# Attention decode on one Trainium2 core: a unit's scores summed in the bank they are made in

## The chip, the core and the metric

The kernel runs on one core of one Trainium2 chip. Its engines are PE (matrix products), DVE (vector), ACT (scalar), POOL (gpsimd) and SP, whose queue issues nearly all transfers; 16 DMA engines move the data from HBM. PE writes to PSUM, which has banks of 128 rows by 512 fp32 values; everything else lies in SBUF, also with 128 rows (partitions). The metric is the device time of one execution in microseconds. Three runs of the kernel before took 217.59 us in the median (217.28 to 218.31).

## The reference

All values are fp32. Two tokens (batch B = 2, one position each, D = 512) attend with 32 query heads of 128 channels over 8 key/value heads, four query heads to each, over the last 4096 positions of the cache. A gated MLP on the same input makes the gate.

```python
def reference(x, k_cache, v_cache, wq, wo, w_in, w_sp, b_sp, w_out):
    xn = layernorm(x)                                  # 2 x 1 x 512
    q = (xn @ wq) as 2 x 32 x 1 x 128
    k, v = the last 4096 positions of the caches, each head repeated 4 times
    p = softmax(q . k * 128 ** -0.5)
    s = (p . v) as 2 x 1 x 4096 @ wo
    z = gelu(xn @ w_in); z1, z2 = halves of z; z2 = layernorm(z2)
    g = silu((z1 * (w_sp * z2 + b_sp)) @ w_out)
    return x + s * g
```

K and V together are 2 x 8 x 4096 x 128 values each, 33.6 MB apiece. With the weights the kernel reads 89.40 MB.

## The kernel before

The work of attention is cut into eight **units**, one for each pair of key/value heads of a token. A unit's K is 128 partitions by 64 positions by 128 channels (one load of 4096 KB), and its V the same; a partition holds 64 neighbouring positions of one of the two heads.

**Transfers.** `ring` has four slots of 4 MB. `enqueue` (L85) and `advance` (L92) hand the slots out in a fixed order: Wq (two slots), w_in, w_out, K0, K1, V0, K2, V1, K3, and so on to K7, V6, V7, and then the output weights wo in pieces of 16, 8, 4, 1, 1, 1 and 1 blocks. A load is issued on SP's queue as soon as the work that read the slot before it is done: from K3 and V2 on, K of unit n+2 after the four transposes of unit n, and V of unit n+2 after the values product of unit n. The queue takes its loads one after the other.

**A unit's scores.** `turn(u, m)` (L371), for m = 0 to 3, is one DVE transpose of 32x32 blocks over 16 of the 64 positions; it makes `kt`, with three buffers. After it, channels lie within blocks of 32, and a product has to be taken for each quarter of 32 channels (`dq`), with its own stationary operand `q_of(u, dq)`, 32 columns wide. `shares` (L378) takes the four products of one key quarter m, one for each `dq`, each into its own group of 32 rows of one PSUM bank `sh`, with nothing summed; ACT copies the bank to SBUF as `shs`. `add_shares` (L389) then sums the four row groups and puts them in their place with a full-width product by the 0/1 matrix `add_dq`: with `add_dq` shifted by m columns, query column 16a + 4g + h of quarter m lands in row 32g + 16a + 4h + m. Four such products, summed in a bank `s`, make a unit's scores. An fp32 product is two passes on PE, and the profile has a record for each.

**The rest of a unit** is done one unit later. `share_max` (L395) finds the maxima (`m2`, `mg`, `mo`, `mx`, `nb`), `probs` (L410) takes the exponentials on ACT with their sums, `probs_t` transposes them, `values` (L436) makes 16 products with V into four row groups of `acc`, `scale_out` and `collect` gather the result.

**The order** is the program's: the engines' calls go through `InOrder` (L27), and the loop at L493 writes each engine's order out by hand. In a turn of the loop with unit u and the unit before it, prev: transpose 0 and its scores; maximum and exponentials of prev; transpose 1, its scores and the sum of quarter 0; values of prev; transposes, scores and sums of the others; the last sum; gathering of prev. After the loop come the last unit's maximum, exponentials and values (L521 to L536), and then the product with wo (L540 to L556): 28 blocks into `part`, which is copied and spread into `so`, and the last four blocks straight into `so`. Two vector operations and the store end the kernel.

Of the kernel before, what the change touches and what calls it, by code (L numbers as in the profile page):

```python
# [9 lines left out]
F32 = mybir.dt.float32  # L10
AF = mybir.ActivationFunctionType
# [3 lines left out]
P = 128  # L15
HQ, DH = 32, 128
G = 4
# [4 lines left out]
def ap(t, offset, dims):  # L22

    return bass.AP(tensor=t.tensor, offset=t.offset + offset, ap=[list(t.ap[0])] + [list(d) for d in dims])
# [18 lines left out]
def kernel(  # L43
# [13 lines left out]
    nc = tc.nc  # L57
    pe, dve, act, sp = (InOrder(tc, e) for e in (nc.tensor, nc.vector, nc.scalar, nc.sync))
    B, _, D = x.shape
    _, HKV, SK, _ = k_cache.shape  # L60
    W = min(4096, max(256, SK // 4))
    REP = HQ // HKV
# [8 lines left out]
    JC = 512 // 32  # L71
    NCH = J // JC
# [4 lines left out]
    sb = ctx.enter_context(tc.tile_pool(name="sb", bufs=2))  # L77
# [23 lines left out]
    def const(name, *shape):  # L101
        return cst.tile([P, *shape], F32, tag=name, name=name)

    def bank(name, tag):
        return ps.tile([P, 512], F32, tag=tag, name=name, bufs=BANKS[tag])
# [75 lines left out]
    nc.gpsimd.memset(hT, 0.0)  # L181
    x4 = const("x4", DC)
    nc.gpsimd.memset(x4, 0.0)
    add_dq = const("add_dq", NCH - 1 + P)
    nc.gpsimd.memset(add_dq, 0.0)
    sel = const("sel", 56)
    nc.gpsimd.memset(sel, 0.0)
    sel4 = const("sel4", 3 + 32)
# [62 lines left out]
    nc.gpsimd.tensor_mul(perm, ap(rowm, 0, [[1, 32], [0, G]]), ap(grpm, 0, [[0, 32], [1, G]]))  # L251
    perm = perm.rearrange("p h e -> p (h e)")
    for a in range(2):
        nc.gpsimd.tensor_copy(
            ap(add_dq, NCH - 1 + 16 * a, [[32, G], [4, REP]]),
            rowm[:, 16 * a : 16 * a + 16].rearrange("p (g h) -> p g h", g=G),
        )
    am = const("am", 2)
    dve.tensor_reduce(am, rowm.rearrange("p (a x) -> p a x", a=2), axis=AX.X, op=ALU.add)
    negm = const("negm", 2)  # L260
# [33 lines left out]
    def q_of(u, dq):  # L294
        return ap(qbd, (u.n * 4 + dq) * 32, [[1, 32]])
# [74 lines left out]

    def turn(u, m):  # L371

        u.kt[m] = sb.tile([P, JC, DH], F32, tag="kt", name=f"kt{u.n}_{m}", bufs=3)
        dve.transpose(
            u.kt[m].rearrange("p j d -> p (j d)"), u.k[:, JC * m : JC * m + JC, :].rearrange("p j d -> p (j d)")
        )

    def shares(u, m):  # L378

        u.sh = bank(f"sh{u.n}_{m}", "sh")  # L380
        for dq in range(4):
            pe.matmul(
                u.sh[32 * dq : 32 * dq + 32, :], q_of(u, dq), u.kt[m][:, :, 32 * dq : 32 * dq + 32],
                start=True, stop=True,
            )
        u.shs[m] = sb.tile([P, 512], F32, tag="shs", name=f"shs{u.n}_{m}")
        act.activation(u.shs[m], u.sh, AF.Copy)

    def add_shares(u, m):  # L389

        if m == 0:
            u.s = bank(f"s{u.n}", "s")
        pe.matmul(u.s, add_dq[:, NCH - 1 - m : NCH - 1 - m + P], u.shs[m], start=(m == 0), stop=(m == NCH - 1))

    def share_max(u):  # L395
        m2 = sb.tile([P, 2], F32, tag="m2", name=f"m2_{u.n}")
# [95 lines left out]
    last = units[-1]  # L492
    for u in units:  # L493
        turn(u, 0)
        shares(u, 0)
        if old is not None and old.n == NU // B - 1:
            divide(0, gather(0))
        if prev is not None:
            share_max(prev)
            probs(prev)  # L500
        turn(u, 1)
        shares(u, 1)
        add_shares(u, 0)
        if prev is not None:
            probs_t(prev)
            weigh(prev)
            if u is not last:
                values(prev)
        for m in range(2, NCH):
            turn(u, m)  # L510
            shares(u, m)
            add_shares(u, m - 1)
        if u is not last and prev is not None:
            scale_out(prev)
        advance(u.slot["k"])
        add_shares(u, NCH - 1)
        if u is not last and prev is not None:
            advance(prev.slot["v"])
            collect(prev)
        old, prev = prev, u  # L520
# [68 lines left out]
```

## Time and profile before

| What | Before |
|---|---|
| Three runs, median (lowest to highest) | 217.59 us (217.28 to 218.31) |
| Profiled execution, first to last instruction (span) | 215.6 us |
| Runs' median less the span | 2.0 us |
| Busy: PE, DVE, ACT, POOL | 144.9, 107.1, 43.7, 4.2 us |
| Read from HBM | 89.40 MB, 415 GB/s over the span |
| Mean granted clock of PE | 0.885 |

The profiled execution has no time of its own on the page beside its span, so the span is set against the runs' median: 2.0 us lie outside it. The DMA row of the page counts how busy the 16 DMA engines are in 40 equal slices of the span, in tenths. A row of a group of instructions gives line, engine, operation, the tile written and those read, shapes and count, then busy time and the mean of one in ns, and the idle time of the engine just before them with what ended it. In a timeline a row begins with its start and its length in us. A row of a window gives the stretch, busy times of PE, PE's weight loads, DVE, ACT and POOL with counts, PE's granted clock, the DMA engines' share and GB/s. All operations stand under line 37, the helper that issues them, so they are told apart by their tiles.

### The profile page before, as it was taken

Reading aid. Unit: us, or ns where it says so; the run is one execution under the profiler, and the core shown is the slowest. Engines: PE = TensorE matmul, PEld = TensorE weight load, DVE = VectorE, ACT = ScalarE, POOL = GpSimd, SP = SyncE. Lnnn points to the kernel's source line nnn. Section 1 sums busy time; section 2 is a strip of 40 time slices with the busy share of each in tenths; the row PEclk is TensorE's granted clock in tenths of the full one; section 3 lists DMA queues with packets and bytes.
Section 4 is the critical chain, followed back from the end, with each engine's and each line's share of the span. In section 5 each row is a group of like instructions: output and inputs, shape, how many; then the busy total and the mean of one; then the engine's idle time right before and its main releaser. Section 6 shows DMA issues by size and latency. Waiting matters only on the chain.

```text
span 215.6 us, 2181 instructions
## 1 busy us (share of the span) xinstructions
PE 144.9 (67%) x848; PEld 40.3 (19%) x848; DVE 107.1 (50%) x161; ACT 43.7 (20%) x108; POOL 4.2 (2%) x22
## 2 busy tenths in 40 slices
PE   0010787224595897699599499459949967987663
PEld 0010222100021222122122132112202211222311
DVE  1140025633995943953936663793585089233101
ACT  2030000331124115114303304130331231241001
POOL 6010000000000000000000000000000000000000
PEclk9999999658599699699799789859975996999998
DMA  9898999999999999999999999999999999999990
GB/s 389 390 389 389 431 423 459 435 438 421 450 395 474 395 453 419 444 432 425 439 404 450 419 444 429 432 432 419 444 413 447 425 432 444 425 435 404 410 376 33
DMA packets 3788, 89.52 MB, mean 415 GB/s; under 512 B 434, under 2 KB 450, under 8 KB 964
## 3 DMA queue, kind: packets, MB, share of 16 engines
q1 hardware_dynamic: 3772, 89.40, 96.9%
q8 instruction: 6, 0.10, 0.2%
q14 instruction: 2, 0.02, 0.0%
q10 hardware_dynamic: 8, 0.00, 0.0%
HBM read 89.40 MB, written 0.00 MB: 415 GB/s over the span
## 4 chain that ended last, share of the span: by engine, by line
DMA 41%; PE 39%; DVE 16%; ACT 2%; issue 2%; DVEq 0%
DMA ring<-in_A_wo_dram 20%; PE sh L37 11%; DMA ring<-in_A_k_cache_dram 11%; DVE kt L37 10%; DMA ring<-in_A_wq_dram 10%; PE s L37 10%; PE acc L37 7%; PE q_ps L37 4%; PE y L37 2%; PE z L37 1%; PE col L37 1%; PE mo L37 1%; DVE gate L37 1%; DVE u L37 1%; DVE qm L37 1%
## 5 line engine op out<-in xcount | busy, mean ns | idle before, releaser
L37 DVE STREAM_TRANSPOSE kt<-ring 128x2048 f32<-128x2048 f32 x32 | 72.2, 2286 | 24.9 <-DMA ring<-in_A_k_cache_dram 24.9
L37 PE MATMUL sh<-kt,qbd 128*32 128x512 f32 x256 | 43.6, 725 | 27.0 <-DVE kt L37 27.0
L37 ACT ACTIVATE shs<-sh 128x512 f32<-128x512 f32 x32 | 19.1, 597 | 99.4 <-PE sh L37 99.4
L37 PE MATMUL s<-shs,add_dq 128*128 128x512 f32 x64 | 39.0, 716 | 0.0
L37 PE MATMUL acc<-ring,pT 128*32 128x512 f32 x256 | 31.3, 614 | 0.0
L37 PEld LDWEIGHTS s<-shs,add_dq 128*128 128x128 f32 x64 | 11.0, 215 | 30.9 <-issue 26.5
L37 PEld LDWEIGHTS sh<-kt,qbd 128*32 128x32 f32 x256 | 7.0, 117 | 46.3 <-issue 38.3
L37 PE MATMUL q_ps<-ring,xnT 128*32 128x512 f32 x64 | 8.8, 713 | 7.6 <-DMA ring<-in_A_wq_dram 7.6
L37 PEld LDWEIGHTS acc<-ring,pT 128*32 128x32 f32 x256 | 7.8, 112 | 22.3 <-issue 17.6
L37 DVE TENSOR_REDUCE m<-s 128x2 f32<-128x512 f32 x8 | 5.4, 680 | 13.0 <-PE s L37 12.9
L37 PE MATMUL xnT_ps<-ident,xn 2*128 2x2 f32 x4 | 0.6, 252 | 14.5 <-DVE xn L37 14.5
L37 ACT ACTIVATE o<-acc,diag 128x128 f32<-128x128 f32 x30 | 8.6, 374 | 4.9 <-PE acc L37 4.9
L37 PE MATMUL part<-ring,oT 128*32 128x512 f32 x56 | 6.6, 597 | 3.5 <-DMA ring<-in_A_wo_dram 3.5
L37 ACT ACTIVATE p<-s,nb 128x256 f32<-128x256 f32 x16 | 7.6, 488 | 6.6 <-DVE nb L37 6.4
L37 DVE STREAM_TRANSPOSE qT<-q_ps 128x512 f32<-128x512 f32 x2 | 1.4, 717 | 14.4 <-PE q_ps L37 14.3
L37 PE MATMUL col<-o,sel 128*32 128x512 f32 x14 | 7.3, 601 | 0.0
L37 DVE TENSOR_TENSOR res<-so,gate 128x128 f32<-128x128 f32 x1 | 0.3, 292 | 11.5 <-PE so L37 11.5
L37 DVE STREAM_TRANSPOSE pT<-p 128x512 f32<-128x512 f32 x8 | 5.4, 674 | 1.2 <-ACT p L37 1.2
L37 PE MATMUL y<-ring,hT 128*32 128x512 f32 x14 | 3.3, 996 | 3.8 <-DVE hT L37 3.8
L37 ACT ACTIVATE zs<-z 128x448 f32<-128x448 f32 x1 | 0.5, 544 | 24.7 <-PE z L37 24.7
L37 ACT ACT_TABLE_LOAD x4 | 5.1, 1283 | 0.8 <-PEq L575 0.7
L37 PEld LDWEIGHTS q_ps<-ring,xnT 128*32 128x32 f32 x64 | 2.5, 130 | 13.1 <-issue 13.1
(114 smaller groups left out, 62.2 us busy)
## 6 DMA issues: line engine op xcount, KB each, us to landing
ring<-in_A_k_cache_dram SPq DMA_DIRECT2D x8, 4096.0 KB, 20.0
ring<-in_A_v_cache_dram SPq DMA_DIRECT2D x8, 4096.0 KB, 28.1
ring<-in_A_wo_dram SPq DMA_DIRECT2D x1, 4096.0 KB, 33.2
ring<-in_B_w_in_dram SPq DMA_DIRECT2D x1, 3584.0 KB, 17.1
ring<-in_A_wo_dram SPq DMA_DIRECT2D x1, 2048.0 KB
ring<-in_B_w_out_dram SPq DMA_DIRECT2D x1, 1792.0 KB, 21.0
ring<-in_A_wo_dram SPq DMA_DIRECT2D x1, 1024.0 KB
ring<-in_A_wo_dram SPq DMA_DIRECT2D x4, 256.0 KB, 17.6
```

What stands on the lines that cost most here:

```text
L37: return self.tc.keep_in_program_order(call(*args, **kwargs))
```

## The change

A unit's score products now all go into one bank. `scores(u, ms)` takes the place of `shares`: for each channel quarter `dq` and each key quarter m of `ms` a product goes into row group m of the unit's `sh`, and the four `dq` are summed there by the accumulation of PSUM. It is called twice a unit, with m = 0, 1 after transpose 1 and with m = 2, 3 after transpose 3. `by_key_group(u)` takes the place of the four `add_shares`: one ACT copy of the full bank and one product by the 0/1 matrix `regroup`, which moves row 32m + 16a + 4g + h to row 32g + 16a + 4h + m of `s`, the place that it had before. `regroup` is copied from columns of the identity on gpsimd, where `add_dq` was cleared and filled. `kt` has four buffers instead of three. Nothing else is changed; the transfers on SP's queue stand in the same order with the same waits.

```diff
-    add_dq = const("add_dq", NCH - 1 + P)
-    nc.gpsimd.memset(add_dq, 0.0)
+    regroup = const("regroup", G, 2, REP, NCH)
...
     for a in range(2):
-        nc.gpsimd.tensor_copy(
-            ap(add_dq, NCH - 1 + 16 * a, [[32, G], [4, REP]]),
-            rowm[:, 16 * a : 16 * a + 16].rearrange("p (g h) -> p g h", g=G),
-        )
+        nc.gpsimd.tensor_copy(regroup[:, :, a], ap(ident, 16 * a, [[4, G], [1, REP], [32, NCH]]))
+    regroup = regroup.rearrange("p g a h m -> p (g a h m)")
...
-        u.kt[m] = sb.tile([P, JC, DH], F32, tag="kt", name=f"kt{u.n}_{m}", bufs=3)
+        u.kt[m] = sb.tile([P, JC, DH], F32, tag="kt", name=f"kt{u.n}_{m}", bufs=4)
...
-    def shares(u, m):
-
-        u.sh = bank(f"sh{u.n}_{m}", "sh")
+    def scores(u, ms):
+
+        if ms[0] == 0:
+            u.sh = bank(f"sh{u.n}", "sh")
         for dq in range(4):
-            pe.matmul(
-                u.sh[32 * dq : 32 * dq + 32, :], q_of(u, dq), u.kt[m][:, :, 32 * dq : 32 * dq + 32],
-                start=True, stop=True,
-            )
-        u.shs[m] = sb.tile([P, 512], F32, tag="shs", name=f"shs{u.n}_{m}")
-        act.activation(u.shs[m], u.sh, AF.Copy)
-
-    def add_shares(u, m):
-
-        if m == 0:
-            u.s = bank(f"s{u.n}", "s")
-        pe.matmul(u.s, add_dq[:, NCH - 1 - m : NCH - 1 - m + P], u.shs[m], start=(m == 0), stop=(m == NCH - 1))
+            for m in ms:
+                pe.matmul(
+                    u.sh[32 * m : 32 * m + 32, :], q_of(u, dq), u.kt[m][:, :, 32 * dq : 32 * dq + 32],
+                    start=(dq == 0), stop=(dq == 3),
+                )
+
+    def by_key_group(u):
+
+        sh = sb.tile([P, 512], F32, tag="shs", name=f"shs{u.n}")
+        act.activation(sh, u.sh, AF.Copy)
+        u.s = bank(f"s{u.n}", "s")
+        pe.matmul(u.s, regroup, sh, start=True, stop=True)
...
         turn(u, 0)
-        shares(u, 0)
...
         turn(u, 1)
-        shares(u, 1)
-        add_shares(u, 0)
+        scores(u, (0, 1))
...
         for m in range(2, NCH):
             turn(u, m)
-            shares(u, m)
-            add_shares(u, m - 1)
+        scores(u, (2, 3))
...
-        add_shares(u, NCH - 1)
+        by_key_group(u)
```

How the order moves, at three places. The digits behind a tile's name are the unit and the key quarter, and then a running number of the buffer. First PE's order in unit 1, before; `x4` is four products in a row:

```order
L37 MATMUL s0_299<-shs0_3_318,add_dq_85 128x512
L37 MATMUL sh1_0_325<-kt1_0_323,qbd_196 32x512 x4
L37 MATMUL mo0_336<-mg0_334,same_r_128 128x16
L37 MATMUL sh1_1_349<-kt1_1_347,qbd_196 32x512 x4
L37 MATMUL s1_356<-shs1_0_330,add_dq_85 128x512
L37 MATMUL acc0_360<-ring_64,pT0_358 32x512 x16
```

And in the changed kernel, from the same place:

```order
L37 MATMUL s0_308<-shs0_306,regroup_85 128x512
L37 MATMUL mo0_316<-mg0_314,same_r_127 128x16
L37 MATMUL sh1_329<-kt1_0_310,qbd_195 32x512
L37 MATMUL sh1_329<-kt1_1_327,qbd_195 32x512
L37 MATMUL sh1_329<-kt1_0_310,qbd_195 32x512
```

The scores of key quarter 0 have moved behind the maximum's product `mo` of the unit before, to those of quarter 1, and the two alternate, eight products in all ahead of `acc`. Second, PE's order in unit 7 from the scores of its third quarter on, before:

```order
L37 MATMUL sh7_2_872<-kt7_2_870,qbd_196 32x512 x4
L37 MATMUL s7_866<-shs7_1_864,add_dq_85 128x512
L37 MATMUL sh7_3_882<-kt7_3_880,qbd_196 32x512 x4
L37 MATMUL s7_866<-shs7_2_877,add_dq_85 128x512
L37 MATMUL s7_866<-shs7_3_887,add_dq_85 128x512
L37 MATMUL acc6_892<-ring_64,pT6_868 32x512 x8
```

And changed, from the last two of its eight products:

```order
L37 MATMUL sh7_767<-kt7_2_778,qbd_195 32x512
L37 MATMUL sh7_767<-kt7_3_780,qbd_195 32x512
L37 MATMUL s7_793<-shs7_791,regroup_85 128x512
L37 MATMUL acc6_795<-ring_64,pT6_776 32x512 x8
L37 MATMUL mo7_808<-mg7_806,same_r_127 128x16
```

One product by `regroup` stands where four by `add_dq` stood between the scores. Third, DVE's order at the start of the units, with what its instructions wait for, before:

```order
L37 STREAM_TRANSPOSE kt0_0_281<-ring_64 128x2048 [waits DMAHW6_49,DMAHW0_49]
L37 STREAM_TRANSPOSE kt0_1_290<-ring_64 128x2048
L37 STREAM_TRANSPOSE kt0_2_301<-ring_64 128x2048
L37 STREAM_TRANSPOSE kt0_3_311<-ring_64 128x2048 [waits DVE_49,PE_49]
L37 STREAM_TRANSPOSE kt1_0_323<-ring_64 128x2048 [waits DMAHW7_49,DVE_49,PE_49]
L37 TENSOR_REDUCE m2_0_332<-s0_299 128x2 [waits PE_49]
```

And changed:

```order
L37 STREAM_TRANSPOSE kt0_0_280<-ring_64 128x2048 [waits DMAHW6_49,DMAHW0_49]
L37 STREAM_TRANSPOSE kt0_1_282<-ring_64 128x2048
L37 STREAM_TRANSPOSE kt0_2_293<-ring_64 128x2048
L37 STREAM_TRANSPOSE kt0_3_295<-ring_64 128x2048
L37 STREAM_TRANSPOSE kt1_0_310<-ring_64 128x2048 [waits DMAHW7_49,DVE_49,PE_49]
L37 TENSOR_REDUCE m2_0_312<-s0_308 128x2 [waits PE_49]
```

The fourth transpose has lost its wait for PE; the fifth waits for PE as before, now for the product that frees the buffer of quarter 0.

## The prediction

> **What bounds the kernel now.** I read the page first: the span, the row of DMA slices and the queue table.
>
> ```profile
> span 215.6 us, 2181 instructions
> DMA  9898999999999999999999999999999999999990
> q1 hardware_dynamic: 3772, 89.40, 96.9%
> ```
>
> The 16 DMA engines are busy in every slice but the last: 89.40 MB pass through one queue, and its packets fill 96.9% of the engines' span. PE stands at 67% and DVE at 50%. Next the chain of waits, at its end:
>
> ```profile
> 168.72 33.24 DMA ring<-in_A_wo_dram
> 201.98 9.97 DMA ring<-in_A_wo_dram
> 211.99 0.47 PE so L37 x8
> ...
> 212.81 0.29 DVE res L37
> ```
>
> From 168.72 to 211.95 the chain is transfer alone; then come one product, two vector operations and the store, 3.7 us to the end of the span. So the last byte sets the end, and a change on PE or ACT moves it in two ways only: it lets the queue run empty, or it makes the work behind the last byte late. The waits say who is ahead in the steady state:
>
> ```profile
> DVE kt L37 <- DMA ring<-in_A_k_cache_dram: 24.9, 5, 8.0
> PE part L37 <- DMA ring<-in_A_wo_dram: 3.5, 3, 1.7
> ```
>
> In the later units the transposes of K wait for K to land, up to 8.0 us; compute is ahead of the transfers there. I looked for the moment of least cover in the windows from the start to each issue of a K load:
>
> ```profile
> 0.00:75.84 75.84, 34.58 (x206) 9.92 (x210) 34.65 (x74) 12.43 (x23) 4.19 (x22) 0.86 0.99 422
> 0.00:92.76 92.76, 48.72 (x278) 13.65 (x282) 45.45 (x83) 16.89 (x35) 4.19 (x22) 0.87 0.99 423
> 0.00:109.70 109.70, 62.89 (x354) 17.39 (x358) 56.35 (x93) 21.34 (x47) 4.19 (x22) 0.88 0.99 424
> 25.00:210.00 185.00, 139.73 (x796) 38.15 (x788) 102.58 (x140) 39.97 (x102) 0.00 (x0) 0.87 1.00 429
> ```
>
> The last number is GB/s. K of unit 3 goes out at 75.84, when the fourth transpose of unit 1 has freed its slot. Issued before it: Wq 8.39 MB, w_in 3.67, w_out 1.84 and five loads of 4.19, together 34.87 MB. Delivered: 422 GB/s by 75.84 us, 32.0 MB. So 2.9 MB are still queued, 6.7 us at 429 GB/s. The same sum gives 4.0 MB or 9.4 us at K of unit 4 (92.76) and 5.1 MB or 12.0 us at K of unit 5 (109.70). A unit needs 8.39 MB, 19.6 us of transfer.
>
> **The change, part by part.** Removed per unit: three of four ACT copies and three of four full-width products. The groups they come from, and the others I use:
>
> ```profile
> L37 PE MATMUL s<-shs,add_dq 128*128 128x512 f32 x64 | 39.0, 716 | 0.0
> L37 ACT ACTIVATE shs<-sh 128x512 f32<-128x512 f32 x32 | 19.1, 597 | 99.4 <-PE sh L37 99.4
> ```
>
> 24 copies of 0.597 us, 14.3 us of ACT, and 24 products of two passes each; in a row one product takes about 1.06 us, so some 25 us of PE. Neither lies on the DMA chain, so neither is a gain by itself. The gpsimd work at the start loses a memset and keeps two copies of other shape, long before their first reader at 68 us: nothing.
>
> Moved: the 16 score products of a unit. Before, four in a row went to four row groups of a bank. Now eight in a row alternate between two groups, and each group sums four products of two passes. How fast such a half is, the trace shows in another product:
>
> ```profile
> 74.46 3.64 PE L37 MATMUL acc<-ring,pT 128*32 128x512 f32 x32
> 77.92 1.04 PE L37 MATMUL sh<-kt,qbd 128*32 128x512 f32 x8
> 82.92 0.59 PE L37 MATMUL col<-o,sel 128*32 128x512 f32 x1
> 83.05 0.63 PE L37 MATMUL sh<-kt,qbd 128*32 128x512 f32 x3
> 83.35 0.59 PE L37 MATMUL col<-o,sel 128*32 128x512 f32 x1
> ```
>
> The values product puts eight passes of 512 columns on each of four groups in 3.64 us; a half puts eight on each of two. The score products now take 1.04 us for two passes on each of four. At 83.05 three passes of the next unit's scores start beside the first pass of `col`, before its second at 83.35: a group has its own line of work, and groups run beside each other. So a half should take 3.6 us at full clock, two halves 7.2 a unit, where four quarters took 4 x 1.0 and four sums 4 x 1.06. The bounds: no shorter, since a group holds eight passes; 7.2 if the two groups ran one after the other. I take 3.6, the nearest row being of the same passes and widths.
>
> [...]
>
> Where this lies on a path: **first unit**.
>
> ```profile
> 53.87 11.07 DVE L37 STREAM_TRANSPOSE kt<-ring 128x2048 f32<-128x2048 f32 x5
> 58.51 1.93 PE L37 MATMUL sh<-kt,qbd 128*32 128x512 f32 x8 [0.35 <-DVE kt L37]
> 66.50 0.69 DVE L37 TENSOR_REDUCE m<-s 128x2 f32<-128x512 f32 x1 [1.56 <-PE s L37]
> 68.53 2.31 DVE L37 STREAM_TRANSPOSE kt<-ring 128x2048 f32<-128x2048 f32 x1
> 82.96 0.69 DVE L37 TENSOR_REDUCE m<-s 128x2 f32<-128x512 f32 x1 [4.92 <-PE s L37]
> 85.44 2.31 DVE L37 STREAM_TRANSPOSE kt<-ring 128x2048 f32<-128x2048 f32 x1
> ```
>
> The first half can start where the second quarter does, 58.51. PE comes out of idling there; with 4 us at half clock it does 2.0 of its 3.6 by 62.5 and ends at 64.1. The second half ends 3.6 later, 67.7; copy 0.65 with its hand-over, regrouping 1.1: scores ready at 69.4 instead of 66.5. Queued on DVE behind that wait are the maximum, then the second transpose of unit 1 (68.53 before) and all that follows, K of unit 3 among it: 2.9 us late of 6.7 us of cover. The fourth kt buffer lets the fourth transpose go without waiting, but the fifth now waits for the whole first half; that is inside this sum.
>
> **The loop.** From 68.53 to 85.44 a unit takes 16.9 us. After the change: transpose 2.3 + 0.1, first half 5.4 (3.6 us of it at half clock), values 3.6, second half 3.6, copy and regrouping 1.75, and 2.5 from 82.96 to 85.44: 19.3 us, less where values use the idle groups. It is under the 19.6 of the transfers; each unit loses 2.4 until K is late enough to wait for: 5.3 of 9.4 us of cover at unit 4, 7.7 of 12.0 at unit 5. About 4 us of queue are left each time. No gap in the DMA, cost nothing; without that cover each late microsecond would be one of the kernel's.
>
> **The end.** After unit 7's K no load depends on its scores, but the output does.
>
> ```profile
> 172.86 2.31 DVE L37 STREAM_TRANSPOSE kt<-ring 128x2048 f32<-128x2048 f32 x1 [7.98 <-DMA ring<-in_A_k_cache_dram]
> 179.49 1.67 PE L37 MATMUL sh<-kt,qbd 128*32 128x512 f32 x8 [2.78 <-DVE kt L37]
> 179.86 4.46 DVE L37 STREAM_TRANSPOSE kt<-ring 128x2048 f32<-128x2048 f32 x2
> 188.09 1.92 PE L37 MATMUL acc<-ring,pT 128*32 128x512 f32 x16
> 200.73 0.25 DVE L37 TENSOR_SCALAR oT<-ol,wd 32x32 f32<-32x32 f32 x1
> 202.09 3.64 PE L37 MATMUL part<-ring,oT 128*32 128x512 f32 x32 [1.74 <-DMA ring<-in_A_wo_dram]
> 206.91 1.92 PE L37 MATMUL part<-ring,oT 128*32 128x512 f32 x16 [1.17 <-DMA ring<-in_A_wo_dram]
> 209.41 1.07 PE L37 MATMUL part<-ring,oT 128*32 128x512 f32 x8 [0.58 <-DMA ring<-in_A_wo_dram]
> 211.25 0.42 PE L37 MATMUL so<-parts,rowm 128*32 128x128 f32 x8
> ```
>
> Before, the scores are ready when `acc` starts, 188.09. How long PE is at half clock, the windows give:
>
> ```profile
> 160.00:166.00 6.00, 5.95 (x22) 1.33 (x26) 4.88 (x3) 0.60 (x1) 0.00 (x0) 0.50 1.02 437
> 179.40:183.10 3.70, 3.61 (x12) 0.70 (x12) 3.70 (x3) 0.60 (x1) 0.00 (x0) 0.56 1.03 443
> ```
>
> PEclk stands ahead of the DMA share: 0.56 until 183.1, once 0.50 for six busy microseconds. After the change the first half starts at 179.49, has done 1.8 of 3.6 by 183.1 and ends at 184.9; the second (transposes done at 184.3) ends by 188.5; copy and regrouping 1.75: 190.25, **2.2 us late**. Low bound 1.75, if the second half runs beside the rest of the first; high 3.4, with six microseconds at half clock. [...] What swallows it: attention is ready for the output weights at 200.98 and PE starts on them at 202.09, when they land (1.1 us); then PE waits 1.17 and 0.58 for the next pieces, and at the end 0.3 lie between the spread at 211.25 and the product on the last piece at 211.99. Together 3.15 us. So 2.2 cost nothing, 3.4 cost 0.2. V of unit 6 is weighed 2.2 later, and so the output weights' third load is issued at 194.5 instead of 192.25; it queues behind the first of them, which lands at 201.98 by the chain.
>
> The sum: nothing on the DMA chain, 0 us at the end: a span of 215.6 again, and with the 2.0 us that lie between it and the runs' median, 217.6. PE's and ACT's busy time fall without use.
>
> **The rivals.** *The two groups don't run side by side*: a half is 7.2 at full clock, the loop 2.4 + 9.0 + 3.6 + 7.2 + 1.75 + 2.5 = 26.5 us, over the transfers' 19.6; unit 1's second transpose comes at 78.7, unit 7's six loops later at 237.7 instead of 177.0, and the kernel takes about 275. For it: no row shows two groups alternating. Against: four groups do, and `col` beside three. *The clock stays at half for the whole of unit 7's scores*, since PE idles longer ahead of them: the first half ends at 186.7, the second between 191.7 and 193.9, copy and regrouping at half clock 2.75: 6.4 to 8.6 us late, over the 3.15 from which it decides; 221 to 223. Against it: in no window is PE busy at half clock for over some 6 us. *Less traffic makes the transfers quicker*: over the 29 stretches of 5 us from 55 to 200 of which these are the first and the last, the mean is 431 GB/s where PE is busier than its median and 430 where it is less:
>
> ```profile
> 55.00:60.00 5.00, 3.42 (x16) 0.43 (x16) 5.00 (x3) 0.60 (x1) 0.00 (x0) 0.50 1.03 446
> 195.00:200.00 5.00, 3.85 (x31) 1.65 (x26) 1.92 (x7) 0.63 (x2) 0.00 (x0) 1.00 0.95 410
> ```
>
> So a gain of over 1.1 us (216.4 or less) has nothing behind it. *The change doesn't shorten PE's work* (halves at half clock throughout the loop but not the end) gives the forecast's time too as long as 4 us of cover stand.
>
> **How the numbers follow.** Hidden on both sides: 0.83, 217.6, by itself 217.0 to 218.6 with the end's 0.2 and the runs' spread (217.28 to 218.31). Clock rival 0.06, serial groups 0.03, some other lateness 0.02; quicker transfers 0.06. About 0.5%, 1.1 us, is what a measurement here tells from no change. The range reaches a little to both sides, 216.6 to 219.2. Faster 0.06, same 0.83, slower 0.11.
>
> **What would show it.** In the changed profile: DMA slices full as now; the last transfer's end near 212; s with 16 passes instead of 64 and 8 copies; a half of 16 passes in 3.6 us at full clock; K of unit 3 issued near 78.7; unit 7's regrouping ended near 190; PE's waits for output weights shrunk from 3.5 us by about 2. Wrong would be a gap in the DMA row, K's wait gone in units 5 to 7, or `part` ending after 210.8.

## The result, and the profile after

The changed kernel took 219.36 us in the median of 13 runs (217.53 to 220.67), against 217.59 us for the kernel before on the same chip (217.28 to 218.31): 1.0068 times as long, with an interval from 1.0040 to 1.0096. A second series of both, on another chip, gave 218.78 us against 217.67, 1.0033 (1.0004 to 1.0061). The ratios are those of the means. So the change costs 0.3 to 0.7%, 0.7 to 1.5 us, where no change was forecast. The first median lies 0.2 us above the range that was given (216.6 to 219.2), the second inside it. That they come so near is owed to the width of the range and not to the sum, which had 0 us at the end.

The page of the changed kernel, in the rows shown of the kernel before:

```profile
span 216.1 us, 2016 instructions
DMA  9988999999999999999999999999999999999990
q1 hardware_dynamic: 3772, 89.40, 96.7%
```

The transfers look as they did: full slices, 96.7% of the engines' span against 96.9%. The chain of waits doesn't. On the page of the kernel before its shares were

```profile
DMA 41%; PE 39%; DVE 16%; ACT 2%; issue 2%; DVEq 0%
```

and on the page of the changed kernel they are, with the chain's rows at the end:

```profile
PE 54%; DVE 27%; DMA 10%; ACT 5%; issue 2%; ACTq 0%; DVEq 0%
...
204.96 6.26 PE part L37 x56
211.95 0.91 PE so L37 x24
```

Before, transfers alone made up the chain from 168.72 to 211.95. Now it runs through unit 7's scores and values into one unbroken output product of 56 passes and waits for no piece of wo. The 16 DMA engines are as busy as ever, and yet they no longer set the end. The windows around the last transfer show it, in the kernel before and then in the changed one (the last two numbers are the DMA engines' share and GB/s):

```profile
211.00:212.00 1.00, 0.79 (x26) 0.39 (x19) 0.00 (x0) 0.20 (x1) 0.00 (x0) 1.00 0.13 49
```

```profile
211.00:212.00 1.00, 0.66 (x24) 0.39 (x20) 0.00 (x0) 0.60 (x1) 0.00 (x0) 1.00 0.11 43
212.00:213.00 1.00, 0.82 (x24) 0.55 (x24) 0.12 (x1) 0.00 (x0) 0.00 (x0) 1.00 0.00 0
```

By the packets of the trace the last byte passes at 211.51 us before and at 211.39 after. Behind 212 the changed kernel has 0.82 us of PE's work left, where the chain before had one last product of 0.47 us, begun at 211.99.

What the change removed is gone as counted. The groups of the changed kernel:

```profile
L37 PE MATMUL s<-shs,regroup 128*128 128x512 f32 x16 | 9.0, 643 | 6.1 <-ACT shs L37 6.1
L37 ACT ACTIVATE shs<-sh 128x512 f32<-128x512 f32 x8 | 4.8, 597 | 34.8 <-PE sh L37 34.8
```

ACT fell from 43.7 to 30.1 us. And the vector engine's waits have changed sides:

```profile
DVE m L37 <- PE s L37: 33.8, 7, 6.3
DVE hq L37 <- PE col L37: 6.9, 2, 4.4
DVE kt L37 <- DMA ring<-in_A_k_cache_dram: 2.1, 1, 2.1
```

Before, the transposes waited 24.9 us for K: compute was ahead of the transfers. In this execution they wait 2.1 us for K and 33.8 for scores. Nothing has been lost in the transfers yet, but the lead is gone. Most of that isn't the change's doing: this execution starts its units 3.1 us later than that of the kernel before (57.0 and 53.9), for a reason that the first experiment shows, and a second profile of the same kernel, with an early start, still waits 16.3 us for K:

```profile
DVE kt L37 <- DMA ring<-in_A_k_cache_dram: 16.3, 5, 5.0
```

The first profile's timeline of unit 7 shows where the lead is missed:

```profile
172.75 2.31 DVE L37 STREAM_TRANSPOSE kt<-ring 128x2048 f32<-128x2048 f32 x1 [2.12 <-DMA ring<-in_A_k_cache_dram]
177.29 0.69 DVE L37 TENSOR_REDUCE m<-s 128x2 f32<-128x512 f32 x1 [2.23 <-PE s L37]
179.19 2.31 DVE L37 STREAM_TRANSPOSE kt<-ring 128x2048 f32<-128x2048 f32 x1
181.55 3.83 PE L37 MATMUL sh<-kt,qbd 128*32 128x512 f32 x16 [1.71 <-DVE kt L37]
186.53 3.62 PE L37 MATMUL sh<-kt,qbd 128*32 128x512 f32 x14 [1.15 <-DVE kt L37]
...
190.90 1.12 PE L37 MATMUL s<-shs,regroup 128*128 128x512 f32 x2 [0.75 <-ACT shs L37]
192.06 0.69 DVE L37 TENSOR_REDUCE m<-s 128x2 f32<-128x512 f32 x1 [5.58 <-PE s L37]
204.65 0.25 DVE L37 TENSOR_SCALAR oT<-ol,wd 32x32 f32<-32x32 f32 x1
204.96 6.22 PE L37 MATMUL part<-ring,oT 128*32 128x512 f32 x56 [0.68 <-DVE oT L37]
```

Unit 7's first transpose starts with K's landing, at 172.75, as before (172.86). The second is queued on DVE behind the maximum of unit 6, which waits 2.23 us for unit 6's scores; it starts at 179.19, and at 177.0 in the kernel before. From there to the scores' maximum it is 12.9 us, where it was 11.2 (177.0 to 188.2). 2.2 and 1.7 make attention 3.9 us late for the output weights: 204.9 instead of 200.98. In the second profile, with the early start, the second transpose comes at 178.38, and 1.34 and 1.71 make attention 3.1 us late, at 204.1. The waits of `part` for wo, 3.5 us before, are gone in both.

**The runs.** Of every run the span and PE's mean granted clock were recorded, and they say more than the medians of the times. Of the 85 runs of the kernel before that were made beside the experiments below, 83 have spans from 215.5 to 216.1 us, and two of 216.3 and 216.4. The changed kernel's 25 runs go from 215.7 to 218.9, with 217.4 in the middle, and by the clock they fall into groups: 6 runs at 0.919 to 0.921 have 215.7 to 215.9 us; 8 at 0.913 or 0.914 have 216.1 to 218.9 (seven of them 217.4 or less); 11 at 0.890 to 0.898 have 217.4 to 218.4. In the kernel before, the clock varies too (0.863 to 0.897), and the span doesn't follow it, but for the lowest clock, 0.863, where three runs have 216.1 to 216.4. So the change has laid bare PE's clock, which was hidden behind the transfers.

### The profile page after: what moved, and what is told of

Read it like the earlier page. It is cut to its first block, busy times and chain, and to the rows that moved or that the text cites. A ratio compares the mean times of both kernels' runs of the same rounds, so it can differ in the third digit from the quotient of the medians.

```text
span 216.1 us, 2016 instructions
## 1 busy us (share of the span) xinstructions
PE 148.3 (69%) x800; PEld 40.7 (19%) x800; DVE 107.1 (50%) x161; ACT 30.1 (14%) x84; POOL 4.2 (2%) x21
## 3 DMA queue, kind: packets, MB, share of 16 engines
q1 hardware_dynamic: 3772, 89.40, 96.7%
## 4 chain that ended last, share of the span: by engine, by line
PE 54%; DVE 27%; DMA 10%; ACT 5%; issue 2%; ACTq 0%; DVEq 0%
PE sh L37 23%; DVE kt L37 15%; PE acc L37 11%; DMA ring<-in_A_wq_dram 10%; PE q_ps L37 5%; PE s L37 4%; PE part L37 3%; ACT shs L37 2%; DVE m L37 2%; PE z L37 2%; PE mo L37 2%; PE y L37 2%; DVE mg L37 1%; DVE gate L37 1%; DVE u L37 1%
## 5 line engine op out<-in xcount | busy, mean ns | idle before, releaser
L37 PE MATMUL sh<-kt,qbd 128*32 128x512 f32 x256 | 75.5, 652 | 16.7 <-DVE kt L37 16.7
L37 PE MATMUL acc<-ring,pT 128*32 128x512 f32 x256 | 34.2, 595 | 0.0
L37 PEld LDWEIGHTS sh<-kt,qbd 128*32 128x32 f32 x256 | 16.3, 118 | 65.2 <-issue 35.2
L37 DVE TENSOR_REDUCE m<-s 128x2 f32<-128x512 f32 x8 | 5.5, 691 | 33.8 <-PE s L37 33.8
L37 PE MATMUL q_ps<-ring,xnT 128*32 128x512 f32 x64 | 9.9, 785 | 7.5 <-DMA ring<-in_A_wq_dram 7.5
L37 PE MATMUL s<-shs,regroup 128*128 128x512 f32 x16 | 9.0, 643 | 6.1 <-ACT shs L37 6.1
L37 PEld LDWEIGHTS acc<-ring,pT 128*32 128x32 f32 x256 | 9.2, 109 | 18.0 <-issue 17.9
L37 ACT ACTIVATE shs<-sh 128x512 f32<-128x512 f32 x8 | 4.8, 597 | 34.8 <-PE sh L37 34.8
L37 PE MATMUL mo<-mg,same_r 128*128 128x16 f32 x16 | 3.4, 289 | 3.9 <-DVE mg L37 3.9
L37 DVE TENSOR_REDUCE hq<-col 32x32 f32<-32x128 f32 x8 | 2.3, 282 | 7.0 <-PE col L37 6.9
L37 PEld LDWEIGHTS s<-shs,regroup 128*128 128x128 f32 x16 | 2.4, 188 | 13.3 <-ACT shs L37 11.6
```

The costliest lines, as they stand in the source:

```text
L37: return self.tc.keep_in_program_order(call(*args, **kwargs))
```

## The experiments

The theory: **the transfers keep their time, but the work behind them has lost its cover at the end.** Each late microsecond of attention is free until wo is used up, then counts in full, and the long output product counts its clock on top. The rivals: **the transfers starve** (a K load is issued to an empty queue, because compute is late in the loop), and **a term of PE's work alone**, the score products being more than PE can do in a unit.

**The same kernel again.** No edit; a second profile.

> The changed kernel once more, nothing edited. Theory (the end is now set by the chain of products and vector work, with no cover left, and how late it is depends on where PE is granted half clock): the runs scatter again from about 217.5 to 220.5; in this profile the last transfer ends within 0.5 us of 211.4 whatever the time, and the span less 211.4 grows with the time of unit 7's scores. First rival (the queue of transfers runs dry, at K of unit 3 or 4): in a profile with a span over 217 there is a gap in the transfers and the last one ends at 212.5 or later. Second rival (something fixed behind the last transfer has become longer): every span is longer by the same amount.

Measured: 218.78 us (217.46 to 220.21, 12 runs), 1.0033 (1.0004 to 1.0061); the profiled run has a span of 216.9 us. Its timeline from unit 7's second transpose on, and windows at the end:

```profile
178.38 2.30 DVE L37 STREAM_TRANSPOSE kt<-ring 128x2048 f32<-128x2048 f32 x1
...
202.44 1.03 PE L37 MATMUL ol<-o,sel 128*32 128x128 f32 x8 [1.21 <-DVE o L37]
204.16 7.89 PE L37 MATMUL part<-ring,oT 128*32 128x512 f32 x56 [0.68 <-DVE oT L37]
```

```profile
202.00:204.00 2.00, 1.03 (x8) 0.80 (x8) 0.92 (x5) 0.00 (x0) 0.00 (x0) 1.00 0.96 410
204.00:206.00 2.00, 1.84 (x12) 0.52 (x16) 0.10 (x1) 0.00 (x0) 0.00 (x0) 0.54 1.00 422
```

The output product starts 0.8 us sooner than in the first profile and ends 0.9 us later, since from 204 on PE is granted little over half of the clock (0.54 from 204 to 206 and 0.60 from 206 to 208, where the first profile has 1.00): 7.89 us for what took 6.22. The expectation had tied the span to the time of unit 7's scores; they come 0.8 us sooner here, and the span is 0.8 us longer. And the first profile has its own loss elsewhere, in the part before the units, which the change doesn't touch. There the MLP's product took, before and after the change:

```profile
34.40 3.21 PE L37 MATMUL z<-ring,xnT 128*32 128x448 f32 x32
```

```profile
35.88 4.63 PE L37 MATMUL z<-ring,xnT 128*32 128x448 f32 x32
```

At a lower clock there (0.50 granted from 36 to 38 us, 1.00 in the kernel before) and in what leads up to it, unit 0's first transpose started at 57.0 us instead of 53.9; in this second profile it was 54.3. All fourteen profiles taken fall on one or the other side, with first transposes at 53.2 to 54.7 or at 56.3 to 57.0, or 8 us late in the two whose units stand behind added transposes (below). So there are two places where the clock can cost the changed kernel a microsecond or two, and the groups of runs above would be neither, one, and both. That is read from three profiles (this one and the first with one each, both at 0.913; one further down with both, at 0.890), not from every run, and the run of 218.9 us at 0.914 doesn't fit it.

**Half of the score products.** Unit scores over two of the four channel quarters alone: the kernel leaves out the products of the other two.

```diff
-        for dq in range(4):
+        for dq in range(2):
-                    start=(dq == 0), stop=(dq == 3),
+                    start=(dq == 0), stop=(dq == 1),
```

> The changed kernel with the score products of two of the four channel quarters left out: it computes scores over half the channels. A half takes 1.8 us instead of 3.6. Theory: the loop falls to about 15 us, K is waited for again by unit 4 or 5 (some 15 us in total), unit 7's scores are ready near 188.5, and the time is 217.6 with a scatter under 0.6 us. Rival of the dry queue: the same. Rival of something fixed at the end, or of the new copy and regrouping product: still 219 to 220, as those are untouched.

Measured: 217.51 us (217.31 to 217.67), 0.9983 (0.9963 to 1.0002); all ten spans between 215.5 and 215.9. The lateness is that of the score products as they now stand: with half of them attention is ready at 201.4, and `part` waits for wo again (1.51, 1.16 and 0.61 us). It also says what there is to win: nothing. With much less of PE's work the kernel ends where the kernel before does, at the transfers.

**All four row groups at once.** One call with m = 0 to 3 after the fourth transpose, so that 16 products run in four groups instead of twice eight in two.

```diff
-        scores(u, (0, 1))
...
-        scores(u, (2, 3))
+        scores(u, (0, 1, 2, 3))
```

> The changed kernel with one edit: all 16 score products of a unit are taken after the fourth transpose, so that four row groups are filled side by side instead of two and two. Theory: 32 passes in 3.6 us instead of 7.2, the values product goes ahead of them while DVE still transposes, the loop is 15.4 to 17.2 us instead of 17.6, K is waited for again in the later units, unit 7's scores are ready near 189.7, and the time is 217.6 with a scatter under 0.6 us. If what costs time is the latency from the last transpose to the scores, which is the same here (3.6 + 1.75), the time stays at 219 to 220.

Measured: 217.72 us (217.38 to 219.29), 0.9999 (0.9977 to 1.0021); spans 215.6 to 217.5, 4 of 12 over 216.2. It moves the products' time and the wait with it: the transposes now wait 26.5 us, five times, for the products to free `kt`, since all four buffers are held to a unit's end. Attention was ready at 203.6, 0.5 us before that of the second profile, which has the early start too (1.3 before the first), and one piece of wo was waited for again (0.55 us). No better than the kernel before, and with more scatter than the 0.6 us that were expected.

**Only unit 7 changed, and only units 0 to 6.** Both forms in one program, chosen by unit.

```diff
+    def is_new(u):
+        return u is units[-1]
...
+        if is_new(u):
+            scores(u, (0, 1))
+        else:
+            shares(u, 1)
+            add_shares(u, 0)
```

> Units 0 to 6 take their scores as before the change, unit 7 as after it. Theory (two latenesses add up: unit 6's scores hold up unit 7's second transpose by 2.2 us, unit 7's own are 1.7 us later, and only 3.15 are covered): one alone is hidden, 217.6, unit 7's scores ready at 189.8 to 190.4 and PE waiting for output weights by 1 to 2 us in total. If the end alone costs it, 219 to 220.

The other one turns the condition round, `u is not units[-1]`.

> The other half of the run with only unit 7 changed: units 0 to 6 take their scores as after the change, unit 7 as before it. Theory (two latenesses add up): unit 6's scores hold up unit 7's second transpose to 178.4 to 179.2 instead of 177.1, unit 7's own chain is as before (11.1 us from that transpose to its scores), ready at 189.5 to 190.3 instead of 188.2; covered, so 217.6 with a scatter under 0.8 us. If the loop alone costs it: 219 to 220.

Measured: with unit 7 alone 217.60 us (217.38 to 218.58), 0.9996 (0.9976 to 1.0016), all ten spans 215.6 to 215.8. With units 0 to 6, 217.91 us (217.43 to 220.18), 1.0033 (1.0003 to 1.0063), spans 215.6 to 218.4, 4 of 10 over 216.2. The timelines, first unit 7 alone:

```profile
189.99 0.69 DVE L37 TENSOR_REDUCE m<-s 128x2 f32<-128x512 f32 x1 [5.59 <-PE s L37]
202.89 3.64 PE L37 MATMUL part<-ring,oT 128*32 128x512 f32 x32 [0.69 <-DVE oT L37]
```

Its scores come at 190.0, 1.8 us later than before: the term that the prediction summed (2.2, to 190.25), nearly alone, and it is hidden. Units 0 to 6:

```profile
191.75 0.69 DVE L37 TENSOR_REDUCE m<-s 128x2 f32<-128x512 f32 x1 [5.02 <-PE s L37]
204.59 7.91 PE L37 MATMUL part<-ring,oT 128*32 128x512 f32 x56 [0.68 <-DVE oT L37]
```

Here unit 7 is the old one, and its scores come still later, at 191.75, 3.55 us after those of the kernel before. Carried lateness is 2.4 us of that (unit 7's second transpose starts at 179.45 instead of 177.04); the rest arises in unit 7, where PE is at about half speed until late: eight passes of the scores take 1.94 us at 181.91 and 1.93 at 185.78, and 1.07 only at 188.73 (before, it was 1.10 at 183.09, with a clock of 1.00 from 184 on). This profile has the late start (56.3 us) and the half-clock output product together, and a span of 217.4. That the lateness would be covered was a miss in 4 of 10 runs. Neither half of the change costs what the whole does in the first series, and cover is used by both; but units 0 to 6 alone come to the ratio of the whole in the second, 1.0033.

**Unit 5's gathering later.** In the changed kernel the first token's four units (0 to 3) are gathered at the start of unit 5's turn, ahead of unit 4's maximum on DVE. Here the gathering goes behind unit 4's values, and its division behind unit 5's transposes.

```diff
-        if old is not None and old.n == NU // B - 1:
-            divide(0, gather(0))
...
+        done = old is not None and old.n == NU // B - 1
+        if done:
+            t = gather(0)
...
+        if done:
+            divide(0, t)
```

> The changed kernel with one piece of work moved: the gathering of the first token (reductions of the collected sums on DVE, a product, a division), which stood ahead of unit 4's maximum and waits for unit 4's scores to be out of PE's way, goes behind unit 4's values, and its division behind unit 5's transposes. Theory (the loop without a wait for K takes 16 to 17.5 us and would be on time in unit 7, but unit 5 loses some 4 us there): unit 5's second transpose starts near 140 instead of 143 to 146, unit 6's scores no longer hold up unit 7's second transpose (177.0 to 177.4), unit 7's scores are ready at 189.8 to 190.3, and the time is 217.6 to 218.0. If the gathering doesn't matter: 219 to 220.

Measured: 217.64 us (217.42 to 218.10, 11 runs), 1.0006 (0.9997 to 1.0015); 10 of 11 spans 215.6 to 216.0, the last 216.3. The whole loss is gone, with all the new products in place, so the rival of PE's work alone falls. Unit 5 on DVE, first in the first profile of the changed kernel, then in the second:

```profile
142.00 1.16 DVE L37 TENSOR_REDUCE hq<-col 32x32 f32<-32x128 f32 x4 [4.37 <-PE col L37]
...
146.00 2.31 DVE L37 STREAM_TRANSPOSE kt<-ring 128x2048 f32<-128x2048 f32 x1
```

```profile
139.09 1.16 DVE L37 TENSOR_REDUCE hq<-col 32x32 f32<-32x128 f32 x4 [2.68 <-PE col L37]
...
142.88 2.30 DVE L37 STREAM_TRANSPOSE kt<-ring 128x2048 f32<-128x2048 f32 x1
```

and with the gathering moved:

```profile
137.96 0.69 DVE L37 TENSOR_REDUCE m<-s 128x2 f32<-128x512 f32 x1 [1.63 <-PE s L37]
139.86 2.31 DVE L37 STREAM_TRANSPOSE kt<-ring 128x2048 f32<-128x2048 f32 x1
...
202.85 3.64 PE L37 MATMUL part<-ring,oT 128*32 128x512 f32 x32 [0.68 <-DVE oT L37]
```

`hq` needs `col`, and PE comes to `col` only behind unit 4's scores, which the change has put in one late run; so DVE stands 4.37 us (2.68) with the maximum and the second transpose queued behind. In the profile of the kernel before, the same gathering waits for nothing (its one wait for `col`, 2.5 us, is that of unit 7's at the end):

```profile
136.14 1.13 DVE L37 TENSOR_REDUCE hq<-col 32x32 f32<-32x128 f32 x4
```

The profile with the gathering moved has an early start (54.1 us), so it is to be set beside the second one. Without the wait unit 5's second transpose starts at 139.86, 3.0 us sooner than there and 0.2 us ahead of the kernel before, and unit 7 starts its second transpose at 177.1 again instead of 178.38. DVE's wait for K is nearly the same, 17.0 us against 16.3. The other 3.1 us of the first profile (146.00) go with its late start.

A late start makes this wait in the kernel before as well. The run with six added products, further down, leaves units 0 to 6 of that kernel as they are and started at 56.9 us:

```profile
DVE hq L37 <- PE col L37: 5.7, 2, 3.1
```

(The other 2.5 us of the 5.7 are the wait at the end.) Its unit 7 starts the second transpose at 178.37, 1.3 us late. So a start 3 us late does to the old loop what the change does to an early one, and where both meet it is 2.2 us.

**The gaps at the end filled.** Two products into a spare bank, read by nobody, stand where PE idles between the last values and the output product.

```diff
+    def keep_busy(cols):
+        pe.matmul(spare[:, :cols], same, last.v[:, 0:4, :]...[:, :cols], start=True, stop=True)
+    keep_busy(512)
     divide(last.b, t[early, :], early)
     collect_last(last)
+    keep_busy(256)
```

> The changed kernel with two spare products put into PE's waits at the end (one of 512 columns ahead of the last gathering products, one of 256 ahead of the product with the output weights), into a bank that nothing reads. Theory on the scatter (PE's clock falls to half after the thin stretch from 198 to 204, and the 28 blocks of the output product, 6.2 us at full clock, now start last and have no cover): the clock stays at 1.00 from 204 to 211, the output product takes 6.2 to 6.5 us, and times over 219 become rare; median 217.6 to 218.4. If the scatter comes from the units ahead, it stays: 217.5 to 220.5.

Measured: 217.58 us (217.43 to 218.94, 11 runs), 1.0008 (0.9991 to 1.0025); 9 of 11 spans 215.6 to 215.9, the others 217.0 and 217.2. The timeline:

```profile
203.94 5.36 PE L37 MATMUL part<-ring,oT 128*32 128x512 f32 x48
209.61 1.06 PE L37 MATMUL part<-ring,oT 128*32 128x512 f32 x8 [0.32 <-DMA ring<-in_A_wo_dram]
```

The output product starts 2.9 us later than attention was ready before, runs at full clock (1.00 in every window of 2 us from 196 to 212), catches up with wo, and the kernel ends at 215.8. With the added work most of the loss is gone, though units 0 to 7 are as late as in the second profile of the changed kernel (unit 7's second transpose at 178.2 and 178.4).

**Both together.** The two edits above in one kernel.

> The changed kernel with both remedies, unit 5's gathering moved and the two spare products at the end. Theory: the end is covered and its clock is full, so only the transfers are left: 217.5 with a scatter of at most 0.4 us, the same as before the change. No way is seen by which it would be under 217.3, as the last transfer ends at 211.6 in every profile so far but the one with a gap.

Measured: 217.55 us (217.43 to 218.40, 12 runs), 0.9996 (0.9982 to 1.0011); 11 of 12 spans 215.6 to 216.1. Together they win no more than either; the last byte, at 211.4 to 211.7 in every profile but the two with all units started late, is the floor.

**The kernel before, with unit 7's scores late.** Three or six products by a matrix of zeros stand ahead of the last sum of unit 7, each two passes that add nothing.

```diff
+        if u is last:
+            for _ in range(3):
+                pe.matmul(u.s, zero, u.shs[NCH - 2], start=False, stop=False)
```

> The kernel before the change with three more full-width products, by a matrix of zeros, ahead of unit 7's last sum: unit 7's scores 2.6 us later (near 190.8) and nothing else. By the prediction's 3.15 us of cover at the end: hidden, 217.6. If the cover at the end is smaller: 218 to 220.

With `range(6)`:

> The same with six such products, 5.2 us: scores near 193.4. By a cover of 3.15 us: 2.0 us longer, 219.6, and up to 221 where the output product falls into half clock. If the end has more cover than that: 217.6.

Measured: with three, 218.16 us (217.53 to 219.38), 1.0031 (1.0011 to 1.0051), spans 215.6 to 217.0, 3 of 10 over 216.2; with six, 220.13 us (219.53 to 220.80, 4 runs), 1.0114 (1.0088 to 1.0141). With three, part of the 0.3% lies outside the span (1.77 to 3.07 us in these runs); with six every span is 217.7 or more. So the kernel before, with its loop as it was, loses time by lateness at the end. The timelines, three and then six:

```profile
190.77 0.69 DVE L37 TENSOR_REDUCE m<-s 128x2 f32<-128x512 f32 x1 [6.32 <-PE s L37]
203.61 5.36 PE L37 MATMUL part<-ring,oT 128*32 128x512 f32 x48 [0.68 <-DVE oT L37]
```

```profile
194.73 0.69 DVE L37 TENSOR_REDUCE m<-s 128x2 f32<-128x512 f32 x1 [9.08 <-PE s L37]
207.57 6.21 PE L37 MATMUL part<-ring,oT 128*32 128x512 f32 x56 [0.68 <-DVE oT L37]
```

In the profile with three, attention is 2.6 us later than 200.98 and the span 215.7: free in that execution, which has the early start. In the one with six (which has the late start as well) it is 6.5 us later and the span 218.7, 3.1 us more. So 3.4 us are free at full clock. With that one number, and 1.7 us for a half-clock output product (7.89 less 6.22), the profiles can be summed:

| Kernel | Attention ready, us | Later than before | less 3.4 | Half clock | Sum | Span less 215.6 |
|---|---|---|---|---|---|---|
| Changed, first profile | 204.9 | 3.9 | 0.5 | 0 | 0.5 | 0.5 |
| Changed, second profile | 204.1 | 3.1 | -0.3 | 1.7 | 1.4 | 1.3 |
| Units 0 to 6 changed | 204.5 | 3.55 | 0.15 | 1.7 | 1.85 | 1.8 |
| Four row groups | 203.6 | 2.6 | -0.8 | 0 | hidden | 0.1 |
| Gaps filled | 203.9 | 2.9 | -0.5 | 0 | hidden | 0.2 |
| Before, six products | 207.5 | 6.5 | 3.1 | 0 | 3.1 | 3.1 |

The 3.4 was fitted to the last row; the others are what it gives. Where a profile has the late start, its attention time has it too. If the first profile's kernel has its output product at half clock too, the sum is 0.5 + 1.7, a span of 217.8: among the eleven runs at the lowest clocks (217.4 to 218.4).

**Everything started late.** Seven DVE transposes of 0.67 us into a tile that nobody reads stand ahead of the units, in the kernel before and in the changed one.

```diff
+    late = sb.tile([P, 512], F32, tag="late", name="late", bufs=1)
+    for _ in range(7):
+        dve.transpose(late, ring[:, :512])
     prev = old = None
```

> The kernel before the change with the same seven extra vector transposes (4.7 us) ahead of the first unit that made the changed kernel 222.2. Theory (before the change that lateness has cover in the queue, 6.7 us at K of unit 3, and the loop is on time again within two or three units): K of unit 3 issued at 80.5 to 81.5, no gap in the transfers, unit 7's second transpose at 177.0 as ever, 217.6 with a scatter under 0.8 us. If any late start costs its length: 220 to 222.

> The changed kernel with seven more vector transposes of 0.67 us (4.7 us) ahead of the first unit, which nothing reads. Theory of lost cover: K of unit 3 is issued at 82.8 to 85.6; the queue held 2.9 to 6.0 us there, so it is at the edge of running dry (a gap of 0 to 2 us), and the time is 219 to 221.5. Theory that the loop catches up before the end whatever its start: the same as without the delay, 218.8 to 219.4, and no gap.

Measured: before 220.25 us (219.34 to 220.46, 4 runs), 1.0105 (1.0077 to 1.0133); changed 222.22 us (220.98 to 224.08, 4 runs), 1.0221 (1.0169 to 1.0274). Both are misses: in the kernel before 4.7 us of delay were to be swallowed by 6.7 us of queue, and the changed one is above its 219 to 221.5. But both profiled runs had the late start besides, with first transposes at 61.9 and 61.8 us, 8.0 after the 53.9 of the kernel before. There K of unit 3 now went out at 84.06, with the queue all but empty:

```profile
84.00:85.00 1.00, 1.00 (x15) 0.27 (x10) 1.00 (x2) 0.00 (x0) 0.00 (x0) 1.00 0.00 0
```

and in the changed kernel SP's timeline and the windows:

```profile
85.59 0.54 SPq L37 DMA_DIRECT2D ring<-in_A_k_cache_dram  x1
```

```profile
84.00:85.00 1.00, 1.00 (x16) 0.31 (x14) 1.00 (x1) 0.00 (x0) 0.00 (x0) 1.00 0.00 0
...
86.00:87.00 1.00, 1.00 (x13) 0.29 (x6) 1.00 (x1) 0.00 (x0) 0.00 (x0) 1.00 0.78 229
```

That is what starving looks like: 0 GB/s in a whole microsecond, and a last byte at 214.3 and 215.7 instead of 211.5. In the changed kernel without the delay there is no such window, K of unit 3 goes out at 80.9 us in the late-started profile (78.1 in the other) with 2.9 us (6.0) of queue left by the packets landed, and the last byte comes at 211.4 (211.6). Counted the same way, the kernel before has 5.8 us left with a late start and 8.0 with an early one (the prediction's 6.7 is from a window's mean rate). So the rival of starved transfers falls for the change as it stands, but the change takes 2 to 3 us of that cover. How much of the last bytes' 2.8 and 4.2 us arises at this one gap and how much at later issues was not told apart.

## Where the prediction was right and where it was wrong, step by step

**Right.** What bounds the kernel, for the loop: the transfers never run dry, the DMA row is full, and their last byte stays within 0.2 us. A half of the scores takes 3.62 us at full clock (3.6 forecast), so two row groups run side by side, and the rivals of serial groups and quicker transfers are out. The groups have 16 passes and 8 copies. K of unit 3 goes out at 78.1 us in the profile with the early start (78.7 forecast). Unit 7's own lateness is 1.7 us in both profiles (1.75 to 3.4 forecast, 2.2 taken; PE is at full clock there, from 178 to 190). The cover at the end is 3.4 us (3.15).

**Wrong: where the sum of the end began.** "The change part by part", under the end, let unit 7's scores start at 179.49, as in the kernel before, and added 2.2 us to that. But the paragraph on the loop had just made the units 5.3 and 7.7 us late, and weighed that lateness against the transfers' queue alone; it assumed that waiting for K wipes it out before unit 7. It does for the first transpose (172.75 and 173.03). It doesn't for the second, which is queued on DVE behind unit 6's maximum, and so behind unit 6's scores: that maximum starts at 176.48 in the second profile and 177.29 in the first, instead of 175.1. With an early start, as in the profile that the prediction was read from, this is 1.3 us more, 3.1 with the 1.7: all of the cover of 3.15 that the same paragraph had counted. With the late start it is 2.2, and 3.9 with the 1.7, over that cover. The experiment with unit 7 alone shows the summed part hidden; the one with units 0 to 6 shows the missing part, 2.4 us with a late start.

**Wrong: a wait that the change lengthened in the loop was not looked for.** The gathering of the first token stands ahead of unit 4's maximum in unit 5's turn, and `col` behind the scores on PE. There `hq` waited for nothing before, and with an early start now waits 2.7 us (4.4 with the late one), with DVE's queue behind it. Moving it makes up the whole loss. The loop's own length was over-estimated, 15.8 to 17.7 us a unit (starts of the second transpose at 73.6, 91.3, 108.7 and 124.5) and not 19.3: values run beside the scores, from the maximum to the second transpose it is 1.9 us and not 2.5, and the first half is at full clock in some units (1.00 from 97 to 144 us in the first profile). So the queue was safer than said, and the end was not.

**Wrong: the cover was priced at full clock.** "So 2.2 cost nothing, 3.4 cost 0.2" took the output product as three runs with waits between them, as it was. Without the waits it is one run of 56 passes right behind attention, and its clock counts: 6.2 or 7.9 us. In the second profile that is the loss: 3.1 us of lateness are covered, and the span is 1.3 us longer with the product at half clock. The rival "the clock stays at half" had the right kind of cost in the wrong place, unit 7's scores, which ran at full clock in both profiles. It was given 0.06, and 221 to 223 us, where the runs spread from 217.5 to 220.7.

**Wrong: one execution stood for all.** That a stretch the change doesn't touch starts the units at 53 to 55 or at 56 to 57 us could not be seen in the one profile shown, but of that spread of 3 us some 0.8 is left at unit 7 of the changed kernel (179.19 against 178.38), where 3.1 of 3.15 us of cover are in use already.

Of the signs that were to show it, "`part` ending after 210.8" came in both profiles (211.2 and 212.0), and "K's wait gone in units 5 to 7", but for 2.1 us, only in the one with the late start.

## What to carry to other kernels

Where transfers bound a kernel, two covers count, and they aren't the same: the queue that is left at each issue, and the time by which the last stage waits for its last pieces. Sum every lateness against both, with the units before the last one included, and ask of each engine's order what is queued behind the instruction that comes late. And when an edit makes waits vanish from the last stage, cost that stage again without them, at the lowest clock that the profile shows for it: waits between products were hiding the clock. And before a wait that has gone or grown is put down to an edit, compare executions that began alike.

## What the runs showed of the hardware

**The clock fell without a long idle stretch.** In the second profile PE's longest rest between 190 us and the output product is 1.21 us (the row at 202.44), and PE is busy for half of 202 to 204 (1.03 us, at a clock of 1.00); yet the clock is 0.54 from 204 to 206. The first profile went through the same stretch at 1.00, with PE less busy:

```profile
202.00:204.00 2.00, 0.79 (x8) 0.78 (x8) 0.79 (x3) 0.46 (x2) 0.00 (x0) 1.00 0.98 418
204.00:206.00 2.00, 1.32 (x15) 0.43 (x17) 0.55 (x2) 0.00 (x0) 0.00 (x0) 1.00 0.94 397
```

So busy time over two microseconds doesn't decide it: 1.03 us of it went ahead of 0.54, and 0.79 ahead of 1.00, in two executions of one program. What does, no run here shows.

**A load issued to an empty queue** moved its first bytes 1.3 us later, in the two runs with all units started late: issue at 85.59, first packets at 86.9 (and 84.06, 85.4 in the kernel before, with 0 GB/s from 84 to 85 and 524 from 85 to 86), by the trace's packets.

**Row groups ran beside each other, but values only beside the end of the scores.** In the changed kernel values start beside the last passes of a half of the scores, on groups that are free:

```profile
80.41 0.63 PE L37 MATMUL acc<-ring,pT 128*32 128x512 f32 x3
80.84 0.59 PE L37 MATMUL sh<-kt,qbd 128*32 128x512 f32 x1
```

They don't start sooner, though two of four groups are free for all of the half and `pT` is ready at 76.49 (75.82 and 0.67 us on DVE): the first pass of values comes at 80.41, 1.0 us before the half ends at 81.43. What holds them back until then, no run here varies.

**The time outside the span varies with the program.** In the 25 runs of the changed kernel 1.73 to 1.84 us lie between the span and the time. In the kernel before it is 1.74 to 3.55 us, and 1.95 or more in 26 of 85 runs. That adds to the spread of its times, not of its spans; what does it was not looked into.
